# Feed-forward products as seven block products for eight, the filter as a complex product, and streamed tables, in a spectral mixing and SwiGLU kernel

## The chip, the cores and the metric

The kernel runs on one core of a Trainium2 chip. Its time is the device time of one launch in microseconds, as the median of several runs. Profiles are of single executions: their span runs from the first to the last instruction.

## The reference

Eight sequences of 3008 tokens with 256 channels are mixed along the sequence by a filter in the frequency domain. Their 24064 rows then pass a gated feed-forward block with a hidden width of 1536. The weights come as float64, everything else as float32, and so is the result.

```python
X = np.fft.rfft(x, axis=1)                     # x: (8, 3008, 256)
Y = X * (filt_r + 1j * filt_i)[None, :, :]     # filters: (1505, 256)
y = np.fft.irfft(Y, n=x.shape[1], axis=1).reshape(24064, 256)
g = y @ w_gate                                 # (256, 1536)
h = g * (1.0 / (1.0 + np.exp(-g))) * (y @ w_val)
out = h @ w_out                                # (1536, 256)
```

## The kernel before

A sequence is taken as 47 x 64 tokens and transformed in two steps. **Stage 1** (line 224, tile pa) does the 47-point transforms, of which a real input needs 24, by one table wf_t; each of its eight loads of x has 94 rows. Its result goes through DRAM (tensor d1), which turns the partition dimension round. **Stage 2** (lines 237 to 260) multiplies each of 24 values of s by its own 128 x 128 table d_t (tile pb), multiplies the result on VectorE with the real and with the imaginary filter, giving two tiles p, and goes back with two matmuls on tables e_t that add up in PSUM (tile pc). The result goes through DRAM again (d2). **Stage 3** (line 271, tile pd) leaves the mixed sequence as tile y with channels on partitions, in eight chunks of 376 tokens for a sequence. Tables and filters are loaded once and stay on chip.

The **feed-forward** part runs over 8 batches x 8 chunks x 12 blocks of 128 hidden columns, 768 steps. In a step, `hidden` makes two products of two matmuls each with 376 moving columns, pg and pv (line 287), takes Silu of pg on ScalarE and multiplies by pv on VectorE, and `project` (line 302) multiplies the hidden block of the step before by 128 x 256 weights, in three tiles of tokens whose PSUM sums stay open for the 12 steps of a chunk.

The order is written by hand: the transforms of batch b + 1 are cut into pieces and put behind given steps of batch b (`at`). Batch 0's transforms run first, with `round_weights` between them: the bits of each float64 weight are turned into the nearest float32 by nine VectorE instructions for each of 18 parts. Thirteen parts are rounded in this start, the other five behind the first feed-forward steps. In the profile an engine's instructions don't always stand in the program's order: VectorE's rounding begins at 33.71 us, before stage 1's last pieces. SP's queue issues loads of x, t and the raw weights, GpSimd's queue the stores, ScalarE's the tables and filters.

Of the kernel before, what the change touches and what calls it, by code (L numbers as in the profile page):

```python
# [12 lines left out]
"""  # L13
# [19 lines left out]
DFF = 1536  # L33
NCB = C // 128
NM = DFF // 128

N1, N2 = 47, 64
NS, NQ = 24, 64
NR = 2 * N1  # rows of 32 tokens in a sequence
NK = 4 * NS  # (re/im, s, half of n2)  # L40

NW = 4  # tokens of a row that a chunk takes
NCHUNK = 32 // NW
TW = NW * NR  # tokens in a chunk
TILES = [(t, min(128, TW - t)) for t in range(0, TW, 128)]
SG = 4  # values of s in a group
NG = NS // SG


def dft_tables():  # L50
# [13 lines left out]
    # Frequencies above S / 2 are kept as the conjugates of those below.  # L64
# [9 lines left out]
    d = d.reshape(128, NS, 128)  # L74
    f32 = np.float32
    return (wf.reshape(NR, NK).astype(f32), wi.reshape(NK, NR).astype(f32),
            d.astype(f32), np.ascontiguousarray(d.transpose(2, 1, 0)).astype(f32))
# [3 lines left out]
def kernel(  # L81
# [11 lines left out]
    wf_host, wi_host, d_host, e_host = dft_tables()  # L93
    wf_dram = nc.inline_tensor(wf_host, name="wf_tbl")
    wi_dram = nc.inline_tensor(wi_host, name="wi_tbl")
    d_dram = nc.inline_tensor(d_host, name="d_tbl")
    e_dram = nc.inline_tensor(e_host, name="e_tbl")
# [9 lines left out]
    ppool = pool("pp", 4)  # L107
# [14 lines left out]
    d_t = cpool.tile([128, NS, 128], FP32)  # L122
    e_t = cpool.tile([128, 2, NS, 128], FP32)
    f_t = [cpool.tile([128, NS, C], FP32, name=f"filt{i}") for i in range(2)]
    wg_t = cpool.tile([128, NCB, DFF], FP32)
    wv_t = cpool.tile([128, NCB, DFF], FP32)
    wo_t = cpool.tile([128, NM, C], FP32)

    flip = [0]

    def evac(dst, src):
        flip[0] ^= 1
        if flip[0]:
            nc.scalar.copy(out=dst, in_=src)  # L134
        else:
            nc.vector.tensor_copy(out=dst, in_=src)  # L136

# [1 line left out]

    def weight_parts():  # L140
        """Views of the weights' bits and where they go, by blocks of 256 of the hidden width."""
        bits = [w.bitcast(U32) for w in (moe_w_gate, moe_w_val)]
        cols = [w.rearrange("(a p) (f two) -> p a f two", p=128, two=2) for w in bits]
        rows = moe_w_out.bitcast(U32).rearrange("(m p) (c two) -> p m c two", p=128, two=2)
        for i in range(DFF // 256):
            for w, dst in zip(cols, (wg_t, wv_t)):
                yield w[:, :, ts(i, 256), :], dst[:, :, ts(i, 256)]
            yield rows[:, ts(i, 2)], wo_t[:, ts(i, 2), :]
# [4 lines left out]
    def load_weights(j):  # L153
        if j < len(weights):
            raws[j] = rpool.tile([128, 2, 256, 2], U32, name=f"raw_{j}", tag="raw")
            nc.sync.dma_start(out=raws[j], in_=weights[j][0])

    def round_weights(j):
        """dst = (-1)^sign * 2^(e - 1023) * (1 + high / 2^20 + low / 2^52): the bracket is rounded
        to 24 bits, and the power, kept to float32's range, is built from its bits."""  # L160
        load_weights(j + 1)
        raw, dst = raws.pop(j), weights[j][1]
        low, high = raw[:, :, :, 0], raw[:, :, :, 1]
        pw = rpool.tile([128, 2, 256], U32, name=f"pw_{j}", tag="pw")
        man = dst.bitcast(U32)
# [6 lines left out]
        v.scalar_tensor_tensor(out=pw, in0=high, scalar=0x80000000, in1=pw,  # L172
                               op0=ALU.bitwise_and, op1=ALU.bitwise_or)
        v.tensor_scalar(out=man, in0=high, scalar1=0xFFFFF, scalar2=None, op0=ALU.bitwise_and)
        v.tensor_scalar(out=dst, in0=man, scalar1=2.0 ** -20, scalar2=1.0,
                        op0=ALU.mult, op1=ALU.add)
        v.scalar_tensor_tensor(out=dst, in0=low, scalar=2.0 ** -52, in1=dst,
                               op0=ALU.mult, op1=ALU.add)
        v.tensor_tensor(out=dst, in0=dst, in1=pw.bitcast(FP32), op=ALU.mult)

# [1 line left out]

    class Spectral:
        """A batch's transforms, in pieces."""

        def __init__(self, b):
            self.b = b
            self.d1 = dpool.tile([2 * NS, N2, C], FP32, name=f"d1_{b}", tag="d1")
            self.d2 = dpool.tile([2 * NS, N2, C], FP32, name=f"d2_{b}", tag="d2")
            self.d1_rows = self.d1.rearrange("a (h n) c -> (a h) n c", h=2)  # L190
            self.d2_rows = self.d2.rearrange("a (h n) c -> (a h) n c", h=2)
            self.x, self.t2, self.p, self.t4 = {}, {}, {}, {}

        def load_x(self, u):
            if u < NCHUNK:
                self.x[u] = xpool.tile([NR, NW, C], FP32, name=f"x_{self.b}_{u}", tag="x")
                nc.sync.dma_start(
                    out=self.x[u],
                    in_=x[self.b].rearrange("(r n) c -> r n c", n=32)[:, ts(u, NW), :])

        def load_t2(self, g):
            if g < NG:
                self.t2[g] = t2pool.tile([128, SG, C], FP32, name=f"t2_{self.b}_{g}", tag="t2")
                for p in range(2):
                    a0 = p * NS + SG * g
                    nc.sync.dma_start(
                        out=self.t2[g][64 * p:64 * p + 64],
                        in_=self.d1[a0:a0 + SG].rearrange("s n c -> n s c"))

        def load_t4(self, u):  # L210
            self.t4[u] = t4pool.tile([NK, NW, C], FP32, name=f"t4_{self.b}_{u}", tag="t4")
            nc.sync.dma_start(out=self.t4[u], in_=self.d2_rows[:, ts(u, NW), :])  # L212

        def stage1(self, u):
            """Over n1, for four of the n2 of each half."""
# [4 lines left out]
            xt = self.x.pop(u)  # L220
            t1 = t1pool.tile([NK, NW, C], FP32, name=f"t1_{self.b}_{u}", tag="t1")
# [204 lines left out]
```

## Time and profile before

| | |
|---|---|
| median of 3 runs | 3567.61 us (3566.69 to 3568.21) |
| span of the profiled execution | 3568.9 us (no time beside the span is recorded for this execution) |
| TensorE: matmul, weight loads busy | 3439.4 us (96%), 2416.4 us (68%) |
| VectorE, ScalarE, GpSimd busy | 788.5, 532.6, 206.4 us |
| mean granted clock of TensorE | 0.995 |

Matmuls are pipelined, so that the mean duration of one is longer than the distance from one to the next; the distance is read from the chain of waits, where groups of the same kind follow each other. Busy shares are means over stages that differ: the first 200 us hold batch 0's transforms, the rest the feed-forward steps with the next batch's transforms between them.

### The profile page before, as it was taken

To read this page: it belongs to the slowest core of one execution; us is meant where nothing else is said; L and a number is where in the kernel's file an instruction comes from. 1 tells how busy PE (TensorE), PEld (TensorE's weight loads), DVE (VectorE), ACT (ScalarE), POOL (GpSimd) and SP (SyncE) were. 2 spreads that over 40 slices of the span, in tenths; PEclk is the share of its full clock that TensorE was granted. 3 is DMA by queue.
4 is the path that set the end of the run, shared out by engine and by line. 5 is a ranking of instruction groups with operands and counts; after the bars stand their busy time and mean duration, and the time that the engine had idled before them with its cause. 6 is when DMAs were issued, how large, how long until landed. Compare 5 with 4: busy or idle time off the path is not lost.

```text
span 3568.9 us, 32112 instructions
## 1 busy us (share of the span) xinstructions
PE 3439.4 (96%) x13184; PEld 2416.4 (68%) x13184; DVE 788.5 (22%) x1418; ACT 532.6 (15%) x1042; POOL 206.4 (6%) x356
## 2 busy tenths in 40 slices
PE   3489999999999999999999999999999999999998
PEld 0356777667776777667776677766777677776776
DVE  2641221112211222112221122211221122211111
ACT  0011111111111111111111111111111111111111
POOL 0000000000000000000000000000000000000000
PEclk9989999999999999999999999999999999999999
DMA  3622111121111210112111211112101111010000
GB/s 126 170 91 68 42 27 30 61 58 43 27 37 61 55 43 17 50 57 56 33 35 44 74 32 37 30 49 70 40 24 35 59 49 44 20 33 14 18 14 9
DMA packets 72771, 167.83 MB, mean 47 GB/s; under 512 B 9520, under 2 KB 35632, under 8 KB 72624
## 3 DMA queue, kind: packets, MB, share of 16 engines
q1 hardware_dynamic: 44416, 84.46, 8.4%
q0 software_dynamic: 24064, 75.00, 7.3%
q10 hardware_dynamic: 4144, 6.33, 0.7%
q8 instruction: 103, 1.69, 0.2%
q14 instruction: 44, 0.36, 0.0%
HBM read 90.77 MB, written 74.97 MB: 46 GB/s over the span
## 4 chain that ended last, share of the span: by engine, by line
PE 83%; issue 11%; POOL 0%; DMA 0%; POOLq 0%; ACT 0%; SPq 0%
PE po L302 24%; PE pg L287 24%; PE pv L287 24%; PE pc L254 4%; PE pd L271 3%; PE pa L224 3%; PE pb L237 2%; POOL out_dram L309 0%; DMA t<-d 0%; DMA d<-g 0%; POOL d L260 0%; POOLq L421 0%; ACT g L134 0%; POOLq L309 0%; SPq L212 0%
## 5 line engine op out<-in xcount | busy, mean ns | idle before, releaser
L302 PE MATMUL po<-wo_t,h 128*128 128x256 f32 (+1 forms) x4608 | 1121.8, 379 | 0.0
L287 PE MATMUL pg<-y,wg_t 128*128 128x376 f32 x3072 | 1096.9, 479 | 0.0
L287 PE MATMUL pv<-y,wv_t 128*128 128x376 f32 x3072 | 1096.7, 479 | 0.0
L302 PEld LDWEIGHTS po<-wo_t,h 128*128 128x128 f32 (+1 forms) x4608 | 859.8, 188 | 258.2 <-issue 28.1
L293 DVE TENSOR_TENSOR h<-s,pv 128x376 f32<-128x376 f32 x768 | 419.7, 547 | 2518.4 <-PE pv L287 2514.7
L287 PEld LDWEIGHTS pv<-y,wv_t 128*128 128x128 f32 x3072 | 584.3, 190 | 387.2 <-issue 1.2
L287 PEld LDWEIGHTS pg<-y,wg_t 128*128 128x128 f32 x3072 | 584.1, 190 | 239.2 <-DVE y L136 0.7
L291 ACT ACTIVATE s<-pg 128x376 f32<-128x376 f32 x768 | 372.4, 485 | 2324.1 <-PE pg L287 2320.7
L224 PE MATMUL pa<-x,wf_t 94*96 94x512 f32 x256 | 135.3, 653 | 58.5 <-DMA x<-in_x_dram 56.1
L309 POOL DMA_DIRECT2D out_dram<-o x192 | 112.0, 587 | 1368.9 <-DVE o L136 966.0
L254 PE MATMUL pc<-p,e_t 128*128 128x256 f32 x768 | 186.1, 386 | 2.9 <-issue 1.1
L254 PEld LDWEIGHTS pc<-p,e_t 128*128 128x128 f32 x768 | 148.2, 194 | 27.5 <-DVE g L136 2.1
L271 PEld LDWEIGHTS pd<-wi_t,t 96*128 96x128 f32 x1024 | 126.0, 194 | 31.1 <-issue 15.2
L237 PE MATMUL pb<-t,d_t 128*128 128x256 f32 x384 | 103.1, 393 | 43.2 <-DMA t<-d 33.8
L271 PE MATMUL pd<-wi_t,t 96*128 96x94 f32 x1024 | 124.7, 275 | 14.8 <-DMA t<-d 14.8
L242 DVE TENSOR_TENSOR p<-pb,filt 128x512 f32<-128x512 f32 x192 | 123.9, 686 | 23.0 <-PE pb L237 22.9
L224 PEld LDWEIGHTS pa<-x,wf_t 94*96 94x96 f32 x256 | 44.0, 176 | 124.9 <-issue 108.1
L237 PEld LDWEIGHTS pb<-t,d_t 128*128 128x128 f32 x384 | 75.2, 198 | 74.0 <-issue 45.6
L260 POOL DMA_DIRECT2D d<-g x96 | 60.2, 631 | 1118.6 <-ACT g L134 655.7
L227 POOL DMA_DIRECT2D d<-t x64 | 34.0, 532 | 866.2 <-ACT t L134 294.7
L134 ACT COPY g<-pc 128x512 f32<-128x512 f32 x62 | 36.4, 587 | 265.9 <-PE pc L254 237.4
L134 ACT COPY y<-pd 128x376 f32<-128x376 f32 x64 | 53.4, 835 | 137.6 <-PE pd L271 137.6
(32 smaller groups left out, 333.2 us busy)
## 6 DMA issues: line engine op xcount, KB each, us to landing
d<-t POOLq DMA_DIRECT2D x64, 384.0 KB, 7.0
t<-d SPq DMA_DIRECT2D x96, 256.0 KB, 4.0
d<-g POOLq DMA_DIRECT2D x96, 256.0 KB, 3.7
t<-d SPq DMA_DIRECT2D x64, 384.0 KB, 4.6
x<-in_x_dram SPq DMA_DIRECT2D x64, 376.0 KB
out_dram<-o POOLq DMA_DIRECT2D x128, 128.0 KB, 2.0
out_dram<-o POOLq DMA_DIRECT2D x64, 120.0 KB, 2.3
raw<-in_moe_w_gate_dram SPq DMA_DIRECT2D x6, 512.0 KB, 16.3
```

Of the source, the lines that this page charges most:

```text
L134: nc.scalar.copy(out=dst, in_=src)
L224: nc.tensor.matmul(out=ps[0:NK], lhsT=wf_t, rhs=xt[:, n:n + 2, :], start=True, stop=True)
L237: nc.tensor.matmul(out=ps[:, i, :], lhsT=d_t[:, s, :], rhs=self.t2[s // SG][:, s % SG, :], start=True, stop=True)
L242: nc.vector.tensor_tensor(out=pt, in0=ps, in1=f_t[k][:, 2 * u:2 * u + 2, :], op=ALU.mult)
L254: nc.tensor.matmul(out=ps[:, i, :], lhsT=e_t[:, k, 2 * w + i, :], rhs=pr[k][:, i, :], start=(k == 0), stop=(k == 1))
L260: nc.gpsimd.dma_start(out=self.d2[a0:a0 + SG].rearrange("s n c -> n s c"), in_=self.g[64 * p:64 * p + 64])
L271: nc.tensor.matmul(out=psv[:, n, :], lhsT=t4[:, n, ts(cb, 128)], rhs=wi_t, start=True, stop=True)
L287: nc.tensor.matmul(out=ps, lhsT=w[:, cb, ts(m, 128)], rhs=y[:, cb, :], start=(cb == 0), stop=(cb == NCB - 1))
L291: nc.scalar.activation(out=silu, in_=pss[0], func=AF.Silu)
L293: nc.vector.tensor_tensor(out=h, in0=silu, in1=pss[1], op=ALU.mult)
L302: nc.tensor.matmul(out=po[0:n], lhsT=h[:, t0:t0 + n], rhs=wo_t[:, m, :], start=(m == 0), stop=(m == NM - 1))
L309: nc.gpsimd.dma_start(out=rows[t0 // NW:(t0 + n) // NW, ts(k, NW), :], in_=o[0:n])
```

## The change

- **Feed-forward.** Each of the three products is taken as a product of 2 x 2 blocks in seven block products instead of eight (Strassen's scheme in Winograd's form). A chunk now has 752 tokens (four chunks for a sequence) in two halves; tokens, channels and hidden width are halved, so that a step j of 6 covers two 128-blocks of the hidden width, one from each half. The seven sums of weight blocks are made once, in `round_weights`, by ScalarE copies and GpSimd additions. The seven sums of y are made in stage 3 by ScalarE, VectorE and GpSimd, and those of the hidden values in `hidden` by four GpSimd additions. Products that share a sum accumulate in the same PSUM bank: after product 1 the bank is copied out by ScalarE, product 6 is added to it, it is copied again, and so on; VectorE adds the copies to other banks.
- **Projection in bursts.** `project` runs once for three steps, with 7 x 3 x 3 products of 128 moving columns, and closes its sums into SBUF tiles; the second burst of a chunk adds to what the first left, on GpSimd and VectorE.
- **Filter.** VectorE makes the complex product of the spectrum and the filter (three instructions and one GpSimd addition), so that the way back takes one matmul instead of two.
- **Streamed tables.** d, e and the filters don't stay on chip: the filters are put into a DRAM tensor once, and each batch loads table and filter again for two values of s at a time.
- **Sizes and order.** Stage 1 works in sixteen pieces of 2 tokens, its loads are split into 80 and 14 rows, and the evacuations have fixed engines. A hidden step calls `fill` at two places between its products, for half of that step's transform pieces each. All 18 weight parts are rounded before the first feed-forward step, whose tiles take the memory of the rounding's.

The core of the diff (the parts of `round_weights` that are left out take the same nine instructions; the order of the pieces is cut to its schedule):

```diff
+LEFT = {1: 0, 2: 1, 4: 2, 5: 3, 6: 4, 7: 5, 3: 6}
+RIGHT = {1: 0, 2: 1, 3: 2, 4: 3, 5: 4, 6: 5, 7: 6}
+HID = {1: 0, 6: 1, 4: 2, 2: 3, 5: 4, 7: 5, 3: 6}
...
+        e = nc.gpsimd
+        if left:
+            for p, a in ((1, w[:, 0, 0]), (2, w[:, 0, 1]), (4, w[:, 1, 1])):
+                nc.scalar.copy(out=dst[:, LEFT[p]], in_=a)
+            add(e, dst[:, LEFT[5]], w[:, 1, 0], w[:, 1, 1])
+            sub(e, dst[:, LEFT[6]], dst[:, LEFT[5]], w[:, 0, 0])
+            sub(e, dst[:, LEFT[7]], w[:, 0, 0], w[:, 1, 0])
+            sub(e, dst[:, LEFT[3]], w[:, 0, 1], dst[:, LEFT[6]])
...
+                for r in (slice(0, 80), slice(80, NR)):
+                    nc.sync.dma_start(out=self.x[u][r], in_=rows[r, ts(u, NV), :])
+
+        def load_two(self, u):
+            if u < N_TWO:
+                b = self.b
+                ss = ts(u, NV)
+                self.tb[u] = tbpool.tile([128, NV, 2, 128], FP32, name=f"tb_{b}_{u}", tag="tb")
+                nc.sync.dma_start(out=self.tb[u], in_=de_dram[:, ss])
...
+                    nc.sync.dma_start(out=self.f[u][half], in_=f_dram[:, ss])
...
+            nc.vector.tensor_tensor(out=pt, in0=ps, in1=f[:, :, 0, :], op=ALU.mult)
+            nc.vector.scalar_tensor_tensor(out=qt[lo], in0=ps[hi], scalar=-1.0,
+                                           in1=f[hi, :, 1, :], op0=ALU.mult, op1=ALU.mult)
+            nc.vector.tensor_tensor(out=qt[hi], in0=ps[lo], in1=f[lo, :, 1, :], op=ALU.mult)
+            add(nc.gpsimd, pt, pt, qt)
...
+                nc.tensor.matmul(out=ps[:, i, :], lhsT=tb[:, i, 1, :], rhs=pt[:, i, :],
+                                 start=True, stop=True)
...
+            if step == 0:
+                nc.scalar.copy(out=turned(1), in_=psv)
+            elif step == 1:
+                nc.scalar.copy(out=turned(3), in_=psv)
+            elif step == 2:
+                sub(nc.vector, turned(5), psv, turned(1))
+                sub(nc.vector, turned(7), turned(3), psv)
+                sub(nc.gpsimd, block(6), block(3), block(5))
+            else:
+                nc.scalar.copy(out=turned(2), in_=psv)
+                sub(nc.gpsimd, block(4), block(2), block(6))
...
+        def product(z, p, kind, start=True):
+            if start:
+                bk[z][kind] = bank(kind, f"{z}{p}_{name}")[:, 0:TH]
+            nc.tensor.matmul(out=bk[z][kind], lhsT=wt[z][:, j, LEFT[p], :], rhs=y[:, RIGHT[p], :],
+                             start=start, stop=True, skip_group_check=True)
+
+        def step(z, p):
...
+            if p in (1, 6, 7):
+                product(z, p, "A", p == 1)
+                nc.scalar.copy(out=u[(1, 6, 7).index(p)], in_=bk[z]["A"])
+                if p == 7:
+                    add(nc.vector, dst[z][:, 2], u[2], bk[z]["E"])
+            elif p == 5:
+                product(z, p, "E")
+            elif p == 2:
+                product(z, p, "F")
+                add(nc.vector, dst[z][:, 0], u[0], bk[z]["F"])
+            elif p == 4:
+                product(z, p, "A", False)
+                if z == "g":
+                    nc.scalar.activation(out=s[:, 3], in_=bk[z]["A"], func=AF.Silu)
+                else:
+                    nc.vector.tensor_tensor(out=h[:, 3], in0=s[:, 3], in1=bk[z]["A"], op=ALU.mult)
+            else:
+                product(z, p, "E", False)
+                add(nc.vector, dst[z][:, 1], u[1], bk[z]["E"])
+                if z == "g":
+                    nc.scalar.activation(out=s[:, 0:3], in_=s[:, 0:3], func=AF.Silu)
+                else:
+                    nc.vector.tensor_tensor(out=h[:, 0:3], in0=s[:, 0:3], in1=h[:, 0:3],
                                             op=ALU.mult)
...
+        for it in ("g1", "v1", "g5", "v5", "g6", "v6", "", "g2", "g7", "v7", "v2", "",
+                   "g4", "v4", "g3", "v3"):
+            if it:
+                step(it[0], int(it[1]))
+            else:
+                fill()
+
+        e = nc.gpsimd
+        add(e, h[:, 4], h[:, 1], h[:, 2])
+        sub(e, h[:, 5], h[:, 0], h[:, 1])
+        sub(e, h[:, 1], h[:, 4], h[:, 0])
+        sub(e, h[:, 6], h[:, 3], h[:, 1])
+        hids[b, k, j] = h
+
+    def project(b, k, q):
...
+            for t, t0 in enumerate(TOK):
+                for i in range(JB):
+                    nc.tensor.matmul(out=bk[kind][:, t, :], lhsT=hs[i][:, HID[p], t0:t0 + 128],
+                                     rhs=wo_t[:, JB * q + i, RIGHT[p], :],
+                                     start=start and t == 0 and i == 0, stop=True,
+                                     skip_group_check=True)
+
+        def place(i, cb, a, kind):
+            dst = o[i][:, :, ts(cb, 128)]
+            if q:
+                add(nc.gpsimd, dst, dst, u[a])
+                add(nc.vector, dst, dst, bk[kind])
+            else:
+                add(nc.vector, dst, u[a], bk[kind])
+
+        product(1, "A")
+        nc.scalar.copy(out=u[0], in_=bk["A"])
+        product(5, "E")
+        product(6, "A", False)
+        nc.scalar.copy(out=u[1], in_=bk["A"])
+        product(2, "F")
+        place(0, 0, 0, "F")
+        product(7, "A", False)
+        nc.scalar.copy(out=u[2], in_=bk["A"])
+        place(1, 1, 2, "E")
+        product(4, "F4")
+        place(1, 0, 2, "F4")
+        product(3, "E", False)
+        place(0, 1, 1, "E")
...
+        while todo:
+            round_weights(todo.pop(0))
+
+    spool = pool("sp", 2)
+    hpool = pool("hp", JB + 1)
+    upool = pool("up", 2)
+    opool = pool("op", 2)
...
+            for u in range(N_ONE):
+                at(u // 2, lambda u=u: nxt.stage1(u))
+            for u in range(N_TWO + 1):
+                if u:
+                    at(9 + u, lambda u=u: nxt.stage2b(u - 1))
+                if u < N_TWO:
+                    at(9 + u, lambda u=u: nxt.stage2a(u))
...
+            hidden(b, k, j, cur.y[k], fill)
+            if late is not None:
+                project(*late)
+                late = None
+            if j % JB == JB - 1:
+                late = (b, k, j // JB)
```

Here NJ = 6 steps make a chunk, JB = 3 a burst, TH = 376 tokens a half, N_ONE = 16 and N_TWO = 12 pieces of stages 1 and 2.

## Rows read from the trace of the kernel before

**Rows 1.** The page: busy totals, forty slices, DMA traffic.
```profile
PE 3439.4 (96%) x13184; PEld 2416.4 (68%) x13184; DVE 788.5 (22%) x1418; ACT 532.6 (15%) x1042; POOL 206.4 (6%) x356
...
PE   3489999999999999999999999999999999999998
...
PEclk9989999999999999999999999999999999999999
...
DMA packets 72771, 167.83 MB, mean 47 GB/s; under 512 B 9520, under 2 KB 35632, under 8 KB 72624
```

**Rows 2.** The chain of waits: start, length (us), engine, tile, line, instructions.
```profile
194.74 2.56 PE pg L287 x4
197.30 2.39 PE pv L287 x4
...
1992.42 1.26 PE pg L287 x4
1993.68 1.26 PE pv L287 x4
1994.94 1.29 PE po L302 x6
...
1998.77 1.72 PE pa L224 x4
2000.48 1.30 PE po L302 x6
...
2038.32 1.76 PE pd L271 x16
...
2121.42 1.73 PE pc L254 x8
```

**Rows 3.** Groups of instructions: busy us, mean ns; idle before.
```profile
L287 PE MATMUL pg<-y,wg_t 128*128 128x376 f32 x3072 | 1096.9, 479 | 0.0
...
L293 DVE TENSOR_TENSOR h<-s,pv 128x376 f32<-128x376 f32 x768 | 419.7, 547 | 2518.4 <-PE pv L287 2514.7 <-PE po L302 3.6
L291 ACT ACTIVATE s<-pg 128x376 f32<-128x376 f32 x768 | 372.4, 485 | 2324.1 <-PE pg L287 2320.7 <-DVE pw L172 3.3
...
L242 DVE TENSOR_TENSOR p<-pb,filt 128x512 f32<-128x512 f32 x192 | 123.9, 686 | 23.0 <-PE pb L237 22.9
...
L134 ACT COPY y<-pd 128x376 f32<-128x376 f32 x64 | 53.4, 835 | 137.6 <-PE pd L271 137.6
...
L134 ACT COPY g<-pc 128x512 f32<-128x512 f32 x62 | 36.4, 587 | 265.9 <-PE pc L254 237.4 <-DVE wo_t L179 12.2 <-DVE pw L172 11.5
...
L134 ACT COPY o<-po 128x256 f32<-128x256 f32 x64 | 23.9, 373 | 98.6 <-PE po L302 98.6
```

**Rows 4.** Busy time by stretch: us, then clock, DMA share, GB/s.
```profile
0.00:60.00 60.00, 18.80 (x20) 4.62 (x20) 13.30 (x27) 4.20 (x6) 2.40 (x8) 1.00 0.39 123
60.00:120.00 60.00, 11.09 (x12) 2.88 (x12) 14.49 (x31) 1.75 (x3) 2.40 (x4) 1.00 0.42 123
120.00:180.00 60.00, 41.77 (x144) 31.83 (x144) 57.03 (x117) 3.52 (x6) 7.82 (x12) 0.91 0.74 194
180.00:240.00 60.00, 48.96 (x177) 33.59 (x178) 30.66 (x66) 8.95 (x15) 1.06 (x2) 0.84 0.34 104
```

**Rows 5.** Timeline of the start: start, length; idle before and its releaser.
```profile
15.09 3.70 PE L224 MATMUL pa<-x,wf_t 94*96 94x512 f32 x4 [15.09 <-DMA x<-in_x_dram]
...
84.70 3.70 PE L224 MATMUL pa<-x,wf_t 94*96 94x512 f32 x4 [4.36 <-DMA x<-in_x_dram]
...
122.25 3.75 PE L237 MATMUL pb<-t,d_t 128*128 128x256 f32 x8 [33.85 <-DMA t<-d]
...
182.83 0.43 DVE L167 TENSOR_SCALAR pw<-raw 128x512 uint32<-128x512 uint32 x1 [0.36 <-DMA raw<-in_moe_w_val_dram]
...
186.66 0.42 DVE L167 TENSOR_SCALAR pw<-raw 128x512 uint32<-128x512 uint32 x1
...
194.53 2.77 PE L287 MATMUL pg<-y,wg_t 128*128 128x376 f32 x4
```

**Rows 6.** Timeline of the end.
```profile
3556.01 2.75 PE L302 MATMUL po<-wo_t,h 128*128 128x256 f32 x12
...
3558.66 1.73 POOL L309 DMA_DIRECT2D out_dram<-o  x3 [41.66 <-DVE o L136]
```

**Rows 7.** GpSimd's issues, and DMA issues with median us to landing.
```profile
L309 POOL DMA_DIRECT2D out_dram<-o x192 | 112.0, 587 | 1368.9 <-DVE o L136 966.0 <-ACT o L134 400.7 <-DVE h L293 2.1
...
d<-t POOLq DMA_DIRECT2D x64, 384.0 KB, 7.0
t<-d SPq DMA_DIRECT2D x96, 256.0 KB, 4.0
```

**Rows 8.** Timeline of two neighbours in the middle.
```profile
2001.62 1.43 PE L287 MATMUL pg<-y,wg_t 128*128 128x376 f32 x4
...
2003.08 0.48 ACT L291 ACTIVATE s<-pg 128x376 f32<-128x376 f32 x1 [1.98 <-PE pg L287]
```

More of the change, by code (lines that the diff above doesn't have):

```diff
@@ L40 @@
 NK = 4 * NS
-NW = 4
+NH = 4
+NW = 2 * NH
 NCHUNK = 32 // NW
[L44 to L47, printed above, removed]
+TH = NH * NR
+TOK = (0, 128, TH - 128)
+NQB = 2
+JB = NJ // NQB
+NV = 2
+N_ONE = 32 // NV
+N_TWO = NS // NV
+LEFT = {1: 0, 2: 1, 4: 2, 5: 3, 6: 4, 7: 5, 3: 6}
+RIGHT = {1: 0, 2: 1, 3: 2, 4: 3, 5: 4, 6: 5, 7: 6}
+HID = {1: 0, 6: 1, 4: 2, 2: 3, 5: 4, 7: 5, 3: 6}
 def dft_tables():
@@ L154, in load_weights @@
         if j < len(weights):
-            raws[j] = rpool.tile([128, 2, 256, 2], U32, name=f"raw_{j}", tag="raw")
-            nc.sync.dma_start(out=raws[j], in_=weights[j][0])
+            raws[j] = rpool.tile([128, 2, 2, 128, 2], U32, name=f"raw_{j}", tag="raw")
+            for i in range(2):
+                nc.sync.dma_start(out=raws[j][:, i], in_=weights[j][0][:, i])
     def round_weights(j):
         load_weights(j + 1)
[L162 to L165, printed above, removed]
+        raw, (_, dst, left) = raws.pop(j), weights[j]
+        low, high = raw[:, :, :, :, 0], raw[:, :, :, :, 1]
+        pw = rpool.tile([128, 2, 2, 128], U32, name=f"pw_{j}", tag="pw")
+        w = rpool.tile([128, 2, 2, 128], FP32, name=f"w_{j}", tag="w")
+        man = w.bitcast(U32)
         v = nc.vector
@@ L341 @@
-    load_weights(0)
-    todo = list(range(len(weights)))
-    for u in range(NS // 2 + 1):
-        if u % (SG // 2) == 0 and u < NS // 2:
-            load_tables(2 * u // SG)
-            load_filter(2 * u // SG)
-        spec.stage2(u)
-        round_weights(todo.pop(0))
-    nc.scalar.dma_start(out=wi_t, in_=wi_dram.ap())
-    spec.load_t4(0)
-    ys[0, 0] = spec.stage3(0)
-    last = None
+            t1 = t1pool.tile([NK, NV, C], FP32, name=f"t1_{self.b}_{u}", tag="t1")
+            ps = fps.tile([128, NV, C], FP32, name=f"pa_{self.b}_{u}", tag="f")
@@ new lines, in stage3, with turned, block @@
+        def stage3(self, k, step):
+            if step == 0:
+                self.y[k] = ypool.tile([128, 7, TH], FP32, name=f"y_{self.b}_{k}", tag="y")
+            y = self.y[k]
+            cb, i = ((0, 0), (1, 1), (0, 1), (1, 0))[step]
+            ps = fps.tile([128, NV, C], FP32, name=f"pd_{self.b}_{k}_{step}", tag="f")
+            psv = ps.rearrange("p a b -> p (a b)")[:, 0:TH].rearrange("p (n r) -> p n r", n=NH)
+            for n in range(NH):
+                nc.tensor.matmul(out=psv[:, n, :], lhsT=self.t4[k, i][:, n, ts(cb, 128)],
+                                 rhs=wi_t, start=True, stop=True)
+            def turned(p):
+                return y[:, RIGHT[p], :].rearrange("p (r n) -> p n r", n=NH)
+            def block(p):
+                return y[:, RIGHT[p], :]
+            if step == 0:
+                nc.scalar.copy(out=turned(1), in_=psv)
[8 more added lines that the diff above has]
+                sub(nc.gpsimd, block(4), block(2), block(6))
@@ new lines @@
+    nc.sync.dma_start(out=wf_t, in_=wf_dram.ap())
+    for k, filt in enumerate((filt_r, filt_i)):
+        for half in range(2):
+            off, step = (0, 1) if half == 0 else (N1, -1)
+            nc.scalar.dma_start(
+                out=f_dram[32 * half:32 * half + 32, :, k, :],
+                in_=bass.AP(tensor=filt.tensor, offset=filt.offset + off * C,
+                            ap=[[N1 * C, 32], [step * C, NS], [1, C]]))
+    nc.scalar.dma_start(out=wi_t, in_=wi_dram.ap())
+    spec = Spectral(0)
@@ new lines @@
+    with tc.tile_pool(name="raw", bufs=2) as rpool:
+        for u in range(N_ONE):
+            spec.stage1(u)
+        load_weights(0)
+        todo = list(range(len(weights)))
+        for u in range(N_TWO + 1):
+            if u < N_TWO:
+                spec.stage2a(u)
+            if u:
+                spec.stage2b(u - 1)
+            round_weights(todo.pop(0))
+        for i in range(2):
+            spec.load_t4(0, i)
+        for step in range(4):
+            spec.stage3(0, step)
+        while todo:
+            round_weights(todo.pop(0))
```

316 lines of the change are left out of this document (139 added, 177 removed).

## The prediction

> **What bounds the kernel now.** I began with the page's engine totals and its forty slices [rows 1]. The reader is to see that TensorE is busy in nearly every slice at full clock and that the other engines lie under 25%: except at the start, the span is TensorE's own work. "Busy" overstates a pipelined engine, so I took the real price of a pass from the chain of waits in the middle of the run, where one group's start follows the other without a gap [rows 2]. Every float32 product is issued as two passes ([rows 3] count 3072 matmuls on line 287 for pg where the loops make 1536), and a pass costs:
> - 376 columns: 1.263 / 4 = 0.3158 us; 256 columns: 1.295 / 6 = 0.2158, and 1.73 / 8 = 0.2163 in pc; 512 columns: 1.72 / 4 = 0.430. That is 0.84 ns a column.
> - pd moves only 94 columns, which would be 0.079 us, but takes 1.76 / 16 = 0.110. Each pass also loads 128 columns of weights, so 0.110 is read as the load's own rate, with the moving hidden under it.
>
> Last I looked at the start. The stage table shows TensorE at 19, 11, 42 and 49 us of each 60 [rows 4], and the timeline shows why [rows 5]: the eight pa groups of batch 0 start 9.9 us apart on average (15.09 to 84.70), each after a load of x; the first pb waits until 122.25, and the first pg starts at 194.53.
>
> **Check of the model.** Passes after 194.5: 6144 x 0.3158 = 1940; 4608 x 0.2158 = 994; pa 224 x 0.430 = 96; pb and pc 336 and 672 x 0.2163 = 73 and 145; pd 1008 x 0.110 = 111. Together 3359. Add 194.5, 2.4 for the first pg and pv at half clock (2.56 and 2.39 us for four passes) and 10.1 from the last po's end to the end of the span [rows 2, 6]: 3566, against the span's 3568.9. The runs' median is 3567.61, 0.04% under the span; no time beside the span is recorded for the profiled execution. I forecast in the span's terms. 0.2%, 7 us, is about what a measurement of this kernel can tell from no change.
>
> **The change, TensorE first.** Seven block products replace eight.
> - Hidden: per step of two 128-blocks and 752 tokens 14 products, 28 passes of 376 columns. 32 chunks x 6 steps x 28 = 5376 x 0.3158 = 1697.5 (was 1940).
> - Projection: 7 products x 3 token tiles x 3 steps x 2 = 126 passes a burst, 64 bursts = 8064 passes, but of 128 columns. These are no row of the trace: below lies pd's 0.110 (128 columns move in 0.107, so not less), above po's 0.2158, twice the columns. pd has the same load and lies 34 columns off, so I take 0.110: 887 (was 994).
> - Filter on VectorE: pc needs one matmul where it had two; 336 x 0.2163 = 73 (was 145).
> - Stages 1, 2a and 3 keep their passes: 96 + 73 + (1024 - 32) x 0.110 = 109.
>
> Sum after the start: 2935, or 15.29 us for each of 192 steps; 424 less.
>
> [...]
>
> **What must stay hidden.** One step gives the others this work; prices from [rows 3].
> - ScalarE: six copies of 376 from PSUM and one Silu (0.485 each), a Silu of 1128. Copies of 256 and 512 take 0.373 and 0.587, so 0.84 ns an element and 0.16 fixed: the long one takes 1.1. With the burst's copies (3 x 0.48 / 3) and the stages' (16 x 0.58 + 12 x 0.59 + 12 x 0.83 per 24 steps), 6.1 of 15.3.
> - VectorE: six adds and one product at 0.547, a product of 1128 (from 0.547 and 0.686: 1.32), a third of four adds, half of three filter ops (0.69 each), a third of one strided subtraction (0.83): 7.2 of 15.3.
> - GpSimd: four dependent adds of 376, plus 1.7 such for blocks of y, filter sum and second burst; and 2.7 DMA issues of 0.58 [rows 7], 1.55 us. The trace has no GpSimd arithmetic. Below lies VectorE's 0.547, above the slowest 376-element row of any engine, 0.835 (y from pd); neither engine is GpSimd, so for the sum I go beyond both, to twice VectorE's, 1.1: 1.55 + 5.7 x 1.1 = 7.8 of 15.3.
>
> [...]
>
> Do the chains inside a step fit? A product takes two passes, 0.63 us, and an evacuation begins 0.2 us after the last pass is out (pg starts at 2001.62, takes 1.26, Silu starts at 2003.08 [rows 2, 8]). A bank is added to only after its copy. g1 is out at 0.63; its copy waits behind the previous step's long Silu (0.15 to 1.25, after v3) and ends at 1.75; g6, which adds to that bank, comes up after four products, at 2.53. The tightest step has stage 2b in the first gap and 2a in the second (0.87 us of TensorE each). Then v2 is out at 7.2 and 2a's matmuls at 8.05; VectorE filters from 8.25 to 10.05 (3 x 0.60), multiplies v4 until 10.55 and adds g3 until 11.05; the long Silu ends at 12.2, the next g1's copy at 12.7. TensorE is through with this step at 10.57, so the next g6 is due at 13.1. That 0.4 us is the least slack I find. GpSimd's four adds end some 6.5 us after the step, and the burst that needs them comes one whole step (8.84) later. One place has none: in each second burst product 3 waits for p7's copy (0.7), a GpSimd add (1.0) and a VectorE add (0.6), 2.35 us against p4's 1.98, so 0.37 x 32 = 12 us.
>
> DMA: filter and tables are read again for every batch, 96 x 0.75 MB = 72 MB beside 168 [rows 1] in 3.1 ms, 77 GB/s, where 120 to 180 us moved 194 [rows 4]. Loads run a step ahead on SP; hidden.
>
> **The start.** All 18 weight parts must now be rounded before the first step, since the work tiles take over their memory: two parts of nine VectorE ops that ran back to back began 3.83 us apart (182.83 and 186.66 [rows 5]), so 18 x 3.85 + 12 x 3 x 0.60 for the filter (0.69 less the overlap seen there) = 91 us. x comes in loads of 80 and 14 rows. If they still pace stage 1 it ends at 88 as before; if not, TensorE's 16 x 1.85 at half clock, the load before it and the filter's copies ahead of ScalarE's queue end it near 55; 11 more for a store of d and a load of t (7.0 and 4.0 [rows 7]), and from 66 VectorE works off what is left. Three parts were rounded in stage 1 before, so 79 us, and I add 5 for waits on raw: 150. Bounds: 120 (VectorE full from 25 us on) and 195 (nothing gained).
>
> **The end.** The last burst waits for the last step's product and GpSimd chain (2.8), then an add (0.75), six DMA issues where there were three (1.8 more): 10.1 + 5.4 = 15.5.
>
> **Sum.** 150 + 2935 + 2.4 + 12 + 15.5 = 3115.
>
> **Rivals.**
> 1. *Evacuation shows.* Where ScalarE's and VectorE's queues run later than worked out (0.4 us of slack), each step stalls 0.5 to 1 us: 192 x that = 96 to 192, 3211 to 3307. For it: seven evacuations hang on accumulating into the same bank, where before a step had two; against it: 40 to 47% load. 0.25.
> 2. *The 128-column pass costs more.* A quarter of the way to po's price, 0.136: + 210, 3325. 0.07. Load and matmul one after the other, 0.110 + 0.107: 8064 x 0.107 = 863 more, 3978, slower; 0.02, since po's pass has no room for a load.
> 3. *The start is no shorter.* At 195 to 215 (five more roundings behind the old pace): 3160 to 3180. 0.10.
> 4. *GpSimd becomes the bound (slower).* It binds when 1.55 + 5.7 p passes 15.29, at p = 2.4 us an add, and the kernel is slower than before from 192 x 17.7 us, p = 2.8. At 3.2 it would give 192 x 19.8 + 168 = 3970. For it: no row has its price, and it issues the DMAs too; against it: that is over five times VectorE's time. 0.03.
>
> **Chances and range.** The forecast holds 0.52: 3115, its own range 3073 (a start at 120, no burst stall) to 3180 (195, and 20 us of stalls). The range over the cases takes the start's bounds and most of rival 1: 3070 to 3290, which leaves out 2 and 4 and the end of 1. Faster 0.94, slower 0.05 (serial loads and GpSimd), and 0.01 that costs cancel.
>
> **What would show it.** pg-like groups of two passes at 0.63 us and bursts of 126 passes at 13.9 us with no gap confirm the TensorE terms; passes of 0.13 or more in a burst mean rival 2. Idle time of TensorE that ends with a copy on ScalarE or an add on VectorE is rival 1, GpSimd busy above 90% is rival 4. The first hidden product should start near 150. The prediction is wrong if the middle slices fall visibly under full TensorE load.

## The result, and the profile after

The changed kernel takes 3157.59 us (median of 4 runs, 3156.83 to 3161.76) against 3567.86 for the kernel before on the same chip: a ratio of 0.8854, interval 0.8841 to 0.8866. That is inside the range given. The forecast was made in terms of the span: the profiled execution took 3157.85 us, its span is 3156.1, and that is 41 us over the point forecast of 3115.

The page of the changed kernel, to lay beside [rows 1]:

```profile
PE 3047.2 (97%) x15488; PEld 2243.0 (71%) x15488; DVE 1432.8 (45%) x2306; ACT 1144.6 (36%) x2104; POOL 1387.8 (44%) x1644
...
PE   4499999999999999999999999999999999999998
...
PEclk9689999999999999999999999999999999999999
...
DMA packets 118291, 240.78 MB, mean 76 GB/s; under 512 B 21712, under 2 KB 55504, under 8 KB 118096
```

TensorE still fills the middle, with more instructions of fewer columns, while the other three engines have about twice to seven times the work. The chain of waits gives the price of a pass as in [rows 2]:

```profile
1504.26 2.27 PE wE_o L421 x18
...
1515.21 0.63 PE wA_v L357 x2
...
1531.47 1.76 PE pd L315 x16
...
1540.03 2.01 PE wA_o L421 x18
1542.04 2.01 PE wE_o L421 x18
```

A hidden pass costs 0.63 / 2, as before. A burst's pass of 128 columns costs 2.01 / 18 = 0.1117 us, pd's 0.110. The first line is the one group of a second burst that waits: 0.26 us over 2.01. The waits of TensorE (line, releaser; total us, times, longest) list all 32 of these beside the waits of the start:

```profile
PE pa L268 <- ACT t L269: 19.4, 5, 9.4
PE pb L280 <- ACT wo_t L214: 11.4, 1, 11.4
PE pd L315 <- DMA t<-d: 10.5, 1, 10.5
PE pb L280 <- DMA tb<-de_tbl: 9.6, 3, 3.2
...
PE wE_o L421 <- DVE o L148: 7.5, 32, 0.7
```

Nothing but the last line recurs in the steps; the others belong to the start. Groups of instructions (busy us, mean ns; idle before):

```profile
L151 POOL TENSOR_TENSOR h<-h 128x376 f32<-128x376 f32 x576 | 564.9, 981 | 28.8
...
L386 DVE TENSOR_TENSOR h<-s,h 128x1128 f32<-128x1128 f32 x192 | 256.0, 1333 | 125.3 <-ACT s L384 125.2
L148 DVE TENSOR_TENSOR h<-u_v,wE_v 128x376 f32<-128x376 f32 x384 | 209.2, 545 | 28.4 <-ACT u_v L366 5.6 <-PE wE_v L357 0.7
```

Last the stretches, as in [rows 4] (busy us of PE, PEld, DVE, ACT, POOL; clock, DMA share, GB/s), and the middle:

```profile
0.00:60.00 60.00, 29.35 (x32) 7.39 (x32) 20.26 (x45) 13.06 (x29) 16.65 (x36) 1.00 0.77 239
60.00:120.00 60.00, 30.03 (x68) 20.63 (x68) 31.73 (x53) 6.51 (x18) 27.29 (x35) 0.77 0.68 198
120.00:180.00 60.00, 32.22 (x91) 22.18 (x92) 53.46 (x91) 14.92 (x43) 32.05 (x54) 0.66 0.76 208
180.00:240.00 60.00, 55.38 (x245) 37.52 (x244) 29.83 (x50) 23.62 (x45) 23.06 (x31) 0.89 0.15 48
...
1400.00:2700.00 1300.00, 1296.92 (x6735) 965.20 (x6734) 584.19 (x931) 486.89 (x883) 586.50 (x680) 1.00 0.27 76
```

In the middle TensorE is idle for 3.1 of 1300 us. What remains of loss lies in the first 200 us, and there the forecast's start of 150 us went wrong. Its timeline (start, length; idle before and releaser):

```profile
65.42 3.45 PE L280 MATMUL pb<-t,tb 128*128 128x256 f32 x8 [11.41 <-ACT wo_t L214]
...
68.76 0.60 SPq L174 DMA_DIRECT2D raw<-in_moe_w_gate_dram  x1
...
92.58 0.33 SPq L246 DMA_DIRECT2D tb<-de_tbl  x1
...
99.45 0.33 SPq L246 DMA_DIRECT2D tb<-de_tbl  x1
...
106.64 0.95 SPq L174 DMA_DIRECT2D raw<-in_moe_w_val_dram  x2
```

The first pb comes at 65.42, where the forecast had 66. From there VectorE was to work without a gap. But SP, which issues all loads in order, issues no raw weight between 68.76 and 106.64: table loads stand ahead, and each waits until a pc has released a table tile, 6.9 us apart (39.3 us in 11 waits of SP's queue from 60 to 170 us). VectorE has rounded six parts by then, and from 64 to 119 us it rounds one; in the stretches of 20 us it is idle for most of the time (columns as above):

```profile
80.00:100.00 20.00, 10.84 (x24) 7.34 (x24) 6.20 (x9) 1.68 (x4) 7.22 (x9) 0.74 0.69 197
100.00:120.00 20.00, 10.89 (x24) 7.56 (x24) 9.68 (x16) 1.59 (x5) 7.87 (x10) 0.74 0.78 229
```

One line of the source view says when rounding is over (duration ns min/median/max, first and last start in us):

```profile
L203 DVE TENSOR_TENSOR w<-w,pw x11: 678/691/692, 118.9 to 187.0; 128x512 f32<-128x512 f32 x11
```

The last part is rounded at 187; the first hidden product starts at 167.98, but its sums stand behind the roundings in VectorE's queue, and TensorE runs without gaps only from 193.

### The profile page after: what moved, and what is told of

The parts are those of the page before. It is cut to its first block, busy times and chain, and to the rows that moved or that the text cites. A ratio compares the mean times of both kernels' runs of the same rounds, so it can differ in the third digit from the quotient of the medians.

```text
span 3156.1 us, 40788 instructions
## 1 busy us (share of the span) xinstructions
PE 3047.2 (97%) x15488; PEld 2243.0 (71%) x15488; DVE 1432.8 (45%) x2306; ACT 1144.6 (36%) x2104; POOL 1387.8 (44%) x1644
## 4 chain that ended last, share of the span: by engine, by line
PE 83%; POOL 7%; DVE 3%; issue 3%; ACT 1%; DMA 1%; SPq 0%; POOLq 0%; DVEq 0%; ACTq 0%
PE wA_g L357 15%; PE wA_v L357 15%; PE wA_o L421 8%; PE wE_g L357 7%; PE wE_v L357 7%; PE wE_o L421 7%; PE wF_o L421 4%; PE wF_g L357 4%; PE wF_v L357 4%; PE pd L315 4%; POOL o L148 3%; PE pa L268 3%; POOL h L151 3%; PE pb L280 3%; PE pc L297 3%
## 5 line engine op out<-in xcount | busy, mean ns | idle before, releaser
L357 PE MATMUL wA_g<-y,wg_t 128*128 128x376 f32 x1536 | 612.6, 480 | 1.0 <-ACT s L377 1.0
L357 PE MATMUL wA_v<-y,wv_t 128*128 128x376 f32 x1536 | 611.0, 479 | 0.0
L151 POOL TENSOR_TENSOR h<-h 128x376 f32<-128x376 f32 x576 | 564.9, 981 | 28.8
L148 POOL TENSOR_TENSOR h<-h 128x376 f32<-128x376 f32 x192 | 187.7, 978 | 732.1 <-PE wE_v L357 388.7
L357 PEld LDWEIGHTS wA_v<-y,wv_t 128*128 128x128 f32 x1536 | 291.7, 190 | 194.4 <-DVE h L379 11.7
L421 PEld LDWEIGHTS wA_o<-wo_t,h 128*128 128x128 f32 x3456 | 406.3, 192 | 16.3
L421 PE MATMUL wA_o<-wo_t,h 128*128 128x128 f32 x3456 | 417.5, 275 | 0.0
L357 PEld LDWEIGHTS wA_g<-y,wg_t 128*128 128x128 f32 x1536 | 283.0, 190 | 176.7 <-issue 27.4
L357 PE MATMUL wE_g<-y,wg_t 128*128 128x376 f32 x768 | 306.0, 480 | 0.0
L357 PE MATMUL wE_v<-y,wv_t 128*128 128x376 f32 x768 | 305.9, 480 | 0.0
L421 PE MATMUL wE_o<-wo_t,h 128*128 128x128 f32 x2304 | 281.6, 276 | 7.5 <-DVE o L148 7.5
L148 DVE TENSOR_TENSOR s<-u_g,wE_g 128x376 f32<-128x376 f32 x384 | 209.1, 544 | 103.8 <-ACT u_g L366 99.8
```

Of the source, the lines that this page charges most:

```text
L148: eng.tensor_tensor(out=dst, in0=a, in1=b, op=ALU.add)
L151: eng.tensor_tensor(out=dst, in0=a, in1=b, op=ALU.subtract)
L357: nc.tensor.matmul(out=bk[z][kind], lhsT=wt[z][:, j, LEFT[p], :], rhs=y[:, RIGHT[p], :], start=start, stop=True, skip_group_check=True)
L421: nc.tensor.matmul(out=bk[kind][:, t, :], lhsT=hs[i][:, HID[p], t0:t0 + 128], rhs=wo_t[:, JB * q + i, RIGHT[p], :], start=start and t == 0 ...
```

## Experiments

Each kernel is the changed kernel with the edit shown, unless it says otherwise. They were run in three groups, in which the kernel before took 3566.3 to 3567.5 us, so a difference of 1 us between two of them says nothing. Theory A is that SP's order of loads, raw weights behind tables, holds the start.

**Four raw tiles for two.**

```diff
-    with tc.tile_pool(name="raw", bufs=2) as rpool:
+    with tc.tile_pool(name="raw", bufs=4) as rpool:
```

> The changed kernel with four buffers instead of two for the rounding's tiles; nothing else. Theory A (queue): the start was 40 us longer than forecast because in SP's in-order queue the loads of raw weights stand behind table loads that wait for a free buffer, so that VectorE had no part to round between 77 and 112 us. Then parts come early, VectorE rounds during stage 1, the last rounding ends some 20 to 28 us sooner than at 189.5, and the time is 3130 to 3138 us. [...]

3161.30 us. VectorE now rounds early (19.59 of the 20 us from 20 to 40), and nothing is won. GpSimd's timeline shows a cost that no theory had:

```profile
23.03 14.37 POOL L148 TENSOR_TENSOR wv_t<-w 128x128 f32<-128x128 f32 x1 [6.96 <-DVE w L203]
37.36 0.91 POOL L151 TENSOR_TENSOR wv_t<-w 128x128 f32<-128x128 f32 x1
```

This addition takes 0.45 us elsewhere. It lasts as long as VectorE's rounding runs back to back (35 VectorE instructions start in it; the first gap between two of them is at 37.09 us, and the addition ends at 37.40); the stores of stage 1 wait behind it and eleven more additions in GpSimd's queue (the first is issued at 45.06, in the changed kernel at 25.15), and the first pb moves from 65.4 to 83.8. ScalarE is late too: its first copy of stage 1 starts at 27.19 instead of 19.05, behind its own loads of the filter; what that costs no run shows by itself.

**Three table tiles, and both together.** The second edit takes one t2 tile away for the memory.

```diff
-    t2pool = pool("t2", 3)
+    t2pool = pool("t2", 2)
-    tbpool = pool("tb", 2)
+    tbpool = pool("tb", 3)
```

> The changed kernel with three buffers for the streamed tables (and two instead of three for t2, to make room). Theory A: a pair of s in the start takes 6.85 us because a table load waits for the way back of two pairs before; with a third buffer the pairs come at 5 us or less, stage 2 ends some 20 us sooner and raw loads get through sooner too: 3133 to 3148 us. [...]

3145.56 us, 12 less: A holds for this part.

> Both: four rounding buffers and three table buffers. Theory A: the start comes down to the forecast, 35 to 45 us less, 3113 to 3123 us, with the first gapless hidden products near 155. [...]

3145.89 us: no more than the tables alone. A, which asked for 3113 to 3123, is not the whole; the early rounding again delays the first pb (83.5), and GpSimd's addition is held again. This became theory C.

**x in loads of 94 rows, as before the change.**

```diff
-                for r in (slice(0, 80), slice(80, NR)):
-                    nc.sync.dma_start(out=self.x[u][r], in_=rows[r, ts(u, NV), :])
+                nc.sync.dma_start(out=self.x[u], in_=rows[:, ts(u, NV), :])
```

> The changed kernel with each load of x in one piece of 94 rows instead of 80 and 14. If the loads of x paced stage 1, as the prediction had it, stage 1 ends at 88 us or later instead of 56, part of which rounding fills: 3173 to 3193 us. Rival: what paces the start lies behind stage 1 (rounding and tables), so it costs nothing: 3156 to 3163.

3211.25 us, 53.7 more and beyond what was expected. The waits of its TensorE:

```profile
PE pa L267 <- DMA x<-in_x_dram: 48.2, 15, 9.8
```

Stage 1 waits for x again, as it did before (56.1 us in 8 waits there, 7.0 in 2 in the changed kernel). The split into 80 and 14 rows is worth 54 us here; what makes the loads of 94 rows slower was not shown.

**Stage 1's and 2's stores of batch 0 issued by ScalarE; or the weight sums made by VectorE.** Both on top of four raw and three table tiles.

```diff
-            nc.gpsimd.dma_start(out=self.d1_rows[:, ts(u, NV), :], in_=t1)
+            store = nc.gpsimd if self.b else nc.scalar
+            store.dma_start(out=self.d1_rows[:, ts(u, NV), :], in_=t1)
```

The store of g is changed in the same way. The other kernel has instead

```diff
-        e = nc.gpsimd
+        e = nc.vector
```

> The kernel with four rounding buffers and three table buffers, and batch 0's stores of stages 1 and 2 issued by ScalarE instead of GpSimd. In the runs before, one GpSimd addition for the weights took 14.37 us while VectorE rounded without a pause, and stage 1's stores stood behind it in GpSimd's queue, so that the first pb came at 83.5 instead of 65.4. Theory C (held adds): GpSimd's additions wait while VectorE runs back-to-back SBUF instructions, and what the start loses is the queue behind them. Then the first pb is back near 66 with the early rounding kept, and the time falls from 3146 to 3120 to 3132. Theory A (queue on SP alone): 3143 to 3149.

3135.98 us, 9.9 less than without the edit, and 21.6 less than the changed kernel. The addition is still held for 14.37 us, but the stores are no longer behind it (first pb at 69.3). So the wait of the stores behind held additions was real, and worth 10 us.

> The kernel with four rounding buffers and three table buffers, and the weights' 72 block sums made by VectorE instead of GpSimd. It adds 72 x 0.2 to 0.3 = 14 to 22 us to VectorE in the start, but nothing of GpSimd is held any more. Theory C: the first pb near 66, stores at once, 3120 to 3140. Theory A, or VectorE's work as the bound of the start: 3155 to 3170, later by what VectorE took over.

3141.97 us, 3.9 less: VectorE pays with 72 sums of its own (three of them in 0.71 us at 173.65). Neither reaches what C expected. The first pb still comes at 76.5 here, though no weight addition is left on GpSimd: stage 1 waits 8.7 us for a copy by ScalarE, which stands in ScalarE's queue behind the copy of a weight that VectorE hasn't rounded yet. A queue in order delays the start on ScalarE too, and C had left that out.

**The filter of batch 0 loaded once.**

```diff
-                self.f[u] = fpool.tile([128, NV, 2, C], FP32, name=f"f_{b}_{u}", tag="f")
+                if b or not u:
+                    self.f0 = fpool.tile([128, NV, 2, C], FP32, name=f"f_{b}_{u}", tag="f")
+                self.f[u] = self.f0
...
-                    nc.sync.dma_start(out=self.f[u][half], in_=f_dram[:, ss])
+                    if b or not u:
+                        nc.sync.dma_start(out=self.f[u][half], in_=f_dram[:, ss])
```

> The kernel with four raw tiles, three table tiles and batch 0's stores on ScalarE's queue (3136), and of batch 0's filter only the first pair's 0.5 MB is loaded and used for all 12 pairs (batch 0's output is that of a wrong filter; the other batches are computed as before). 22 issues of 0.5 us leave SP's queue, and 5.8 MB of some 38 leave the first 165 us, in which the DMA engines are 79% busy. Theory D (the start is paced by the transfers: their bandwidth, or filter loads that hold SP's queue until VectorE is through with the filter tile): 5.8 MB at 232 GB/s is 25 us, 3108 to 3118. Theory E (each pair is a chain of hand-offs, store of g or d, load of t, that takes its own latency whatever else is moved): 3130 to 3137. In both the time moves with the end of the last rounding.

3115.80 us, 20.2 less than with stores by ScalarE alone: D. The source view of the rounding's last line (counted from 100 us on):

```profile
L203 DVE TENSOR_TENSOR w<-w,pw x7: 677/681/693, 104.2 to 144.7; 128x512 f32<-128x512 f32 x7
```

With the filter loads gone the last rounding is at 144.7, before the forecast's 150, and VectorE is 94% busy from 80 to 140. So the filter's loads paced the start of this kernel. Whether by their bytes, by the time that their issues take on SP, or by a load that holds SP's queue until VectorE has released the filter tile, this run doesn't separate.

Over these runs one rule holds: the start of the last rounding (from the view above) against the median.

| kernel | last rounding, us | time, us | difference |
|---|---|---|---|
| changed | 187.0 | 3157.6 | 2970.6 |
| four raw tiles | 192.4 | 3161.3 | 2968.9 |
| three table tiles | 175.3 | 3145.6 | 2970.3 |
| both | 174.0 | 3145.9 | 2971.9 |
| x in 94 rows | 235.3 | 3211.3 | 2976.0 |
| stores by ScalarE | 166.3 | 3136.0 | 2969.7 |
| sums by VectorE | 172.9 | 3142.0 | 2969.1 |
| filter loaded once | 144.7 | 3115.8 | 2971.1 |

Except for x in 94 rows, 5 us off, the difference is the same within 3 us: a microsecond in the last rounding is a microsecond in the time. The kernel's order has it so, since the tiles of the first step take the rounding's memory.

**Is a burst's pass the load's or the move's?** One kernel moves 64 columns in two of three steps of the burst, the other loads 64 token columns as weights there.

```diff
-                    nc.tensor.matmul(out=bk[kind][:, t, :], lhsT=hs[i][:, HID[p], t0:t0 + 128],
-                                     rhs=wo_t[:, JB * q + i, RIGHT[p], :],
+                    cols = slice(0, 64 if i else 128)
+                    nc.tensor.matmul(out=bk[kind][:, t, cols], lhsT=hs[i][:, HID[p], t0:t0 + 128],
+                                     rhs=wo_t[:, JB * q + i, RIGHT[p], cols],
```

> The changed kernel, but in two of three steps of a burst only 64 of the 128 columns are moved (half of those output columns get a third of their sum). 5376 passes load 128 columns and move 64. If the load's rate is the floor, as read from pd, these stay at 0.110 us and the time at 3145 to 3160. If moving sets the pass (0.0565 for 64): 5376 x 0.054 = 290 us less, 2868. If load and moving follow each other in part, something between.

3146.01 us; its chain of waits still has

```profile
2003.25 2.01 PE wE_o L422 x18
```

Half the columns save nothing in these groups: a pass takes 0.1117 us whether it moves 128 columns or 64, so the moving isn't its floor. That the load of 128 columns is, fits this and pd, but is not shown: no run loads and moves 64 columns in the same pass, which a fixed cost of any pass would leave at 0.11. The 11.6 us by which the run is shorter come from elsewhere: in its order a hidden product stands before the group that waited in second bursts, and the wait is gone (7.5 us), and one group of each burst took 1.95 us, 64 x 0.06 = 4 (that the order sets free the wait is read from the chain, not tested).

The other has

```diff
-                    nc.tensor.matmul(out=bk[kind][:, t, :], lhsT=hs[i][:, HID[p], t0:t0 + 128],
+                    m = 64 if i else 128
+                    nc.tensor.matmul(out=bk[kind][0:m, t, :], lhsT=hs[i][:, HID[p], t0:t0 + m],
```

> The changed kernel, but in two of three steps of a burst only 64 of the 128 token columns are loaded as weights (the other tokens get a third of their sum); all move 128 columns. If moving hides the load, nothing changes: 3145 to 3160. If a pass were load plus moving, the 5376 passes would each lose half a load, 0.054: 2870.

3587.10 us. The chain:

```profile
2001.71 3.00 PE wE_o L422 x18
```

Smaller loads cost more, not less: 1 us in 18 passes, 0.32 for each of three changes of width from 128 to 64 and back (429.5 us over 64 x 7 x 3 of them). Neither theory had this. The starts of single passes in the trace, from 2001.64 to 2002.64 us, show where it lies: between passes that both load 64 they are 0.109 us apart, at a change of width and just behind it 0.16 to 0.21. A pass that loads 64 and moves 128 columns thus takes 0.109, hardly more than moving 128 columns alone would (0.107, an estimate at the 0.84 ns a column of the wider passes), so its load adds next to nothing.

**GpSimd's four hidden additions done twice.**

```diff
-        add(e, h[:, 4], h[:, 1], h[:, 2])
-        sub(e, h[:, 5], h[:, 0], h[:, 1])
-        sub(e, h[:, 1], h[:, 4], h[:, 0])
-        sub(e, h[:, 6], h[:, 3], h[:, 1])
+        for fn, d, x1, x2 in ((add, 4, 1, 2), (sub, 5, 0, 1), (sub, 1, 4, 0), (sub, 6, 3, 1)):
+            for _ in range(2):
+                fn(e, h[:, d], h[:, x1], h[:, x2])
```

> The changed kernel, with each of GpSimd's four hidden adds of a step done twice (the same operands again, the results are the same). In the changed kernel such an add takes 0.981 us, so GpSimd gets 3.9 us more in each step of 15.3 (some 11 instead of 7). Theory (GpSimd has room; its chain ends a step before the burst needs it): no change in the middle, TensorE 97% busy, 3157 to 3165, of which up to 4 us at the end, where the last burst waits for the last step's chain. [...]

3302.31 us, 145 more, where 8 at most were expected. GpSimd is 65% busy, so it is no bound by its load. The waits and then the chain at a second burst:

```profile
PE wE_o L420 <- DVE o L148: 103.8, 32, 5.0
```

```profile
2057.05 0.94 POOL h L148
...
2064.04 0.97 POOL h L151
2065.02 1.91 POOL o L148 x2
...
2066.95 0.57 DVE o L148
...
2067.56 4.21 PE wE_o L420 x18
2071.77 0.93 PE wA_g L357 x2
```

All the new waiting of the steps stands at the one place that the forecast found without slack: the second burst's additions to o stand behind eight hidden additions of the next step in GpSimd's queue. The wait grows from 7.5 to 103.8 us, 96 of the 145. Here TensorE has waited 4.9 us, and the granted clock is 0.50 when the burst goes on, so that its 18 passes take 4.21 us for 2.01:

```profile
2064.00:2066.00 2.00, 0.00 (x0) 0.00 (x0) 0.00 (x0) 0.00 (x0) 1.96 (x3) 0.85 0.00 0
2068.00:2070.00 2.00, 2.00 (x11) 2.00 (x11) 0.46 (x1) 0.00 (x0) 1.24 (x3) 0.50 0.05 20
```

Measured by the distance from one pass to the next against its price, the passes behind the waits lose 48 us over the run, where the changed kernel has 3. With the last rounding, which starts 4 us later (191.2), 96 + 45 + 4 make up the 145.

**The kernel before with the new filter alone.**

```diff
-                    for k in range(2):
-                        nc.tensor.matmul(out=ps[:, i, :], lhsT=e_t[:, k, 2 * w + i, :],
-                                         rhs=pr[k][:, i, :], start=(k == 0), stop=(k == 1))
+                    nc.tensor.matmul(out=ps[:, i, :], lhsT=e_t[:, 0, 2 * w + i, :],
+                                     rhs=pr[:, i, :], start=True, stop=True)
...
```

VectorE's and GpSimd's part of the edit is that of the change.

> The kernel before, with the filter alone as a complex product on VectorE and GpSimd: pc takes one matmul for two, 672 passes fewer after the start, at 0.2163 us a pass 73 fewer for all that lies beyond the first 195 us (TensorE bound). The start itself has three filter operations on VectorE for two in each of 12 pairs (0.69 us each) and a GpSimd add in the path from pb to pc: 0 to 15 us longer. Theory (TensorE's passes are the price everywhere after the start): 3495 to 3515. Rival (the new hand-off from VectorE to GpSimd to TensorE shows in every pair of stage 2): 84 pairs x 1 us or more gives the gain back, 3560 to 3600.

3515.72 us, 0.7 over the range expected. The timeline has the first pg at

```profile
211.83 2.77 PE L290 MATMUL pg<-y,wg_t 128*128 128x376 f32 x4
```

17.3 us later than before [rows 5], where 0 to 15 were expected, and the span is 55.4 shorter (3513.5): behind the start 72.7 are gone, 336 x 0.2163. That it fits to the digit is luck: by the medians the kernel is 51.7 us faster, which leaves 69.0, because the profiled execution of the kernel before was some 3 us longer than its others (spans of 3563.8 to 3567.3 us beside these runs, against 3568.9).

**The best parts together:** four raw and three table tiles, stores by ScalarE, and

```diff
-                add(nc.gpsimd, dst, dst, u[a])
-                add(nc.vector, dst, dst, bk[kind])
+                add(nc.vector, dst, dst, bk[kind])
+                add(nc.gpsimd, dst, dst, u[a])
```

> Four raw tiles, three table tiles and two t2 tiles, batch 0's stores issued by ScalarE, and in the second burst the VectorE add of the bank ahead of the GpSimd add of the stored copy (one sum in another order). The first three gave 3136. The second burst's 18 passes that wait now take 2.27 us against 2.01 without a wait, in 32 bursts 8 us. Theory (the wait is for the GpSimd add that stands ahead of the bank's): 3126 to 3130. Rival (the copy of p7 or VectorE's own queue is what the burst waits for): 3133 to 3138.

3136.36 us, as without the exchange and as the rival had it. The 7.5 us line of waits is gone from its view, but the wait has only moved, to a hidden product behind the burst. The wA_v of such a place starts 0.90 us after the wA_g for 0.63, the next product 0.73 after it:

```profile
2883.67 0.80 PE L359 MATMUL wA_g<-y,wg_t 128*128 128x376 f32 x2
2884.57 0.90 PE L359 MATMUL wA_v<-y,wv_t 128*128 128x376 f32 x2
2885.30 0.80 PE L359 MATMUL wF_g<-y,wg_t 128*128 128x376 f32 x2
```

By 2900 us the kernel is only 2.3 us ahead (the same product of VectorE starts at 2900.52 against 2902.80), and one new stall in the last chunk gives that back:

```profile
2972.21 1.62 PE L359 MATMUL wA_v<-y,wv_t 128*128 128x376 f32 x2 [2.59 <-ACT u_v L368]
```

So 3136 us, without the exchange, is the best version here, 0.8793 of the kernel before (0.8780 to 0.8806).

## Why the prediction was right, and where it was off

**TensorE as the price.** Right. The hidden passes cost 0.63 / 2, and of the filter's 73 us 69 to 73 were found alone. The steps' passes, each at its measured price, come to 2949 us for the 2935 forecast.

**The pass of 128 columns.** The value taken, 0.110, measured 0.1117: 8064 x 0.0017 = 14 us more, which is all of that difference. Loads and moves overlap: in the changed kernel matmuls are busy for 97% of the span and weight loads for 71%, and a load (pd's 0.110) and a move (0.107 at 0.84 ns a column) one after the other, as in rival 2, would have made the pass 0.217.

**The start.** This is the term of the sum that was mis-sized, and the step that failed is "from 66 VectorE works off what is left", with 5 us for waits on raw. The first pb came at 65.42 as forecast, and VectorE had by then rounded six parts, not the three reckoned: by the forecast's own prices 12 x 3.85 + 21.6 = 68 us were left, for an end at 134. The last rounding ended at 187.7 instead. From 66 on VectorE was busy for 88.2 us and idle for 33.5: its raw loads stood behind tables on SP, and the streamed loads, which the forecast called hidden for the steps, were not hidden in the start, where each pair of stage 2 needs them at once. The first hidden product came at 167.98 for 150, and by 200 us TensorE lost 12.4 us more to waits and slow passes, where 2.4 were reckoned. So the start cost 28 us more than forecast, and of the 44.5 us that it was to give 16 came. With the last rounding at 187 it lies near the bound of 195, and the time is 4 us from rival 3's 3160: the time alone would not tell the two apart. One reading is left open: stage 1's passes take 3.70 / 4 us, as reckoned, "at half clock", but the rows have 1.00 for the clock of that stretch.

VectorE was also slower beside GpSimd's additions; from the timeline:

```profile
138.54 2.04 DVE L190 TENSOR_SCALAR pw<-pw 128x512 uint32<-128x512 uint32 x1
```

```profile
139.01 1.27 POOL L148 TENSOR_TENSOR p<-p,q 128x512 f32<-128x512 f32 x1
```

This operation takes 0.41 us elsewhere; here it ends 0.3 us after GpSimd's addition. Seven such instructions between 66 and 188 us took 1.47 to 2.04 us, together some 8 us more than elsewhere; each ran beside a GpSimd addition of 1.13 to 1.50 us and ended 0.3 us after it, the last 0.6. So GpSimd's additions have a share in the 20 us by which VectorE's work exceeded 68.

**The rest of the sum.** In a second burst the group that waits starts 2.40 us after the group before it, for 2.01, and the next product 2.11 after that:

```profile
1501.86 2.17 PE L421 MATMUL wF_o<-wo_t,h 128*128 128x128 f32 x18
...
1504.26 2.27 PE L421 MATMUL wE_o<-wo_t,h 128*128 128x128 f32 x18 [0.23 <-DVE o L148]
1506.37 0.80 PE L357 MATMUL wA_g<-y,wg_t 128*128 128x376 f32 x2
```

The wait is thus 0.39 us for the 0.37 forecast, with 0.10 for slower passes behind it; the 0.23 of the view, 7.5 in all, counts only from the end of the last pass before. The 1.0 us taken for GpSimd's addition in that wait stood in no row; the 128 additions to o took 1.039 on average. All that TensorE loses behind 200 us, by the distances of its passes, is 18 us for the 12 forecast, 15 of them at the second bursts. From the start of TensorE's last pass, at 3147.5, to the end of the span it is 8.6 us, where the end was put at 15.5, some of which now stands in the 18. So 150 + 2.4 + 2935 + 12 + 15.5 = 3115 became 168.0 + 12.4 + 2949 + 18 + 8.6 = 3156: errors of 28, 14, 6 and -7 us. The mechanism of the steps was right; the time lies in the range because the range left room for a start as late as 195.

**What stays hidden.** GpSimd's addition took 0.981 us for the 1.1 assumed, and the loads, 45, 36 and 44%, are near the 47, 40 and 51 worked out. Rival 1 did not come: ScalarE's and VectorE's chains fit in each step. Rival 4's threshold was wrong, though. It was put at 2.4 us an addition, where GpSimd's total load fills a step; the doubled additions, with GpSimd at 65%, cost 145 us by order in its queue and the slow passes behind it.

## What to carry to other kernels

When a kernel is bound by one engine, count its passes and price them by neighbouring rows: that gave 2935 of 2949 us. Price a start by its queues, not by the sum of the engine's work: look at which loads stand behind a tile that isn't free yet. And an engine's margin is not its idle share: the place with no slack decides, and a stall on TensorE can be paid again at a lower clock, as the 4.9 us in the doubled run were (0.50 granted behind them, 4.21 us for 2.01).

## What the runs showed of the hardware

- With four raw tiles a GpSimd addition that takes 0.45 us elsewhere lasted 14.37 us while VectorE's rounding ran back to back, and ended 0.3 us after the first gap in it.
- Changing the width of a weight load between 128 and 64 columns cost some 0.32 us for each pair of changes, while passes that load 64 and move 128 columns follow each other at 0.109 us, and passes that load 128 at 0.1117, whether they move 128 or 64.
- After a wait of 4.9 us in the doubled run the granted clock was 0.50, and 18 passes took 4.21 us for 2.01.
